# Gathering the low bits and the sign of 64-bit weights: 16-bit halves in place of 32-bit words

## The chip, the cores and the metric

The kernel runs on one core of one Trainium2 chip. The metric is the time of one execution in microseconds of the device, and the median of the runs shown is 682.36 us (three runs, 682.13 to 684.18). The core's engines run side by side and meet through semaphores: TensorE (PE, with its weight loads as PEld), VectorE (DVE), ScalarE (ACT), GpSimd (POOL) and SyncE (SP), which issues all of this kernel's DMAs.

## The reference, cut to what matters

```python
# attention: 4 batches, 8 heads, 768 positions, head size 64
k_sum = k.reshape(B, H, nb, block, D).max(axis=3)      # 24 blocks of 32 keys
v_sum = v.reshape(B, H, nb, block, D).mean(axis=3)
scores_l = where(|i - j| < 16, scale * q @ k.T, -1e9)  # a window
scores_s = scale * q @ k_sum.T + log(32)               # the block summaries
a = softmax(concat(scores_l, scores_s)); x = a @ concat(v, v_sum)
# feed-forward: 3072 tokens, 512 -> 2048 -> 512
h = x @ w_in
g = h * tanh(log1p(exp(min(h, 20))))                   # mish
return (g @ w_out).astype(float32)
```

The two weight matrices w_in and w_out arrive in 64-bit floating point (viewed as 64-bit integers), and the kernel makes 32-bit floats of them on the chip before it can multiply with them.

## The kernel before, in words

**Attention** is cut into units: a unit is one chunk of 256 queries of one batch and one pair of heads. There are 12 chunks and 4 pairs, so 48 units. A unit is loaded, scored on PE (lines 293 to 299), masked and reduced to its maximum on DVE (line 308, result `nm`), exponentiated on ACT (line 313, sums `sm`), scaled by the reciprocal of its sum (DVE lines 322 and 323 make `rs`, POOL line 324 multiplies), transposed on PE (line 330, copied out by ACT at line 332), and multiplied with the values on PE (line 348, split into a high and a low part by ACT line 349 and DVE line 350).

**Feed-forward** goes over six groups of 512 tokens (two chunks each) and 16 slices of 128 hidden columns, which gives 96 steps. A step is `ff_in` (12 matmuls, line 362), the activation on ACT (line 369), a split into high and low parts (lines 378 and 380) and, two steps later, `ff_out` (12 matmuls, line 390). Every product is made of three matmuls of high and low parts, so each weight is needed as a high part and a low part.

**Weights** come in 16 pieces of two 128x512 blocks, w_in and w_out in turn. A piece goes through five functions. `load_weight` (line 119) issues two DMAs into one of two staging buffers. `begin_weight` has ACT scale the upper 32-bit words into `f` (line 143) and has DVE gather, in the lower words `x`, what `f` lacks: the top three bits of the low word and the sign (lines 144 and 145). `join_weight` clamps `f` (line 154) and shifts the gathered bits in (line 156). `upper_weight` rounds that to the high part on ACT (line 129), and `lower_weight` subtracts to get the low part on DVE (line 134). `f` has one buffer, so the next piece's line 143 waits for line 134.

**Order.** Nothing reorders the program: each engine executes its instructions in the order in which the code writes them. There are two stages in which weights are prepared. In the first (about 0 to 55 us) the eight attention units of the first group run in a loop over u = 0 to 9: `begin_weight` stands at even u and `join_weight` at odd u, so five pieces are begun there. In the second (about 55 to 153 us), the first group's feed-forward steps run, and every step takes the weights on by one: upper and lower of the piece joined in the step before, then begin and join of the next. The other eleven pieces are begun in steps 0 to 10. A step with an attention unit (the even steps here) has on DVE, one behind the other: line 134, line 308 (four times), lines 144 and 145, lines 322 and 323, lines 154 and 156. A step without one has line 350 or nothing where lines 322 and 323 stand. From 153 us on the weights are ready and the other five groups run.

Of the kernel before, what the change touches and what calls it, by code (L numbers as in the profile page):

```python
# [9 lines left out]
F32 = mybir.dt.float32  # L10
F32R = mybir.dt.float32r
U32 = mybir.dt.uint32
I64 = mybir.dt.int64
AF = mybir.ActivationFunctionType
ALU = mybir.AluOpType
# [29 lines left out]

OFFSET = 112
F32_MAX = (0x47EFFFFF - (OFFSET << 23))
SIGN = 0x80000000


def _as_f32(bits):
    import struct
    return struct.unpack("<f", struct.pack("<I", bits))[0]
# [3 lines left out]
def fused_kernel(ctx: ExitStack, tc: tile.TileContext, q0, qk, kt, v0, vw, vs, w_in, w_out, out):  # L57
    nc = tc.nc
# [20 lines left out]
    for h in range(2):  # L79
        r = slice(h * QT, (h + 1) * QT)  # L80
        nc.gpsimd.affine_select(
            out=base[r, 0:KW], in_=base[r, 0:KW], pattern=[[1, KW]], base=-1,
            channel_multiplier=-1, compare_op=ALU.is_ge, fill=NEG / SCALE)
        nc.gpsimd.affine_select(
            out=base[r, 0:KW], in_=base[r, 0:KW], pattern=[[-1, KW]], base=2 * WIN - 1,
# [28 lines left out]
    def load_weight():  # L114
        if weights:
            w, fc = weights.pop(0)
            t = stage.tile([P, WB, WP], I64, tag="stage", name=f"w{w}_{fc}")
            for k in range(WB):
# [17 lines left out]
    def begin_weight():  # L136

        if loaded:
            w, fc, t = loaded.pop(0)
            words = t.rearrange("p k f -> p (k f)").bitcast(U32).rearrange("p (f two) -> p f two", two=2)  # L140
            x, high = words[:, :, 0], words[:, :, 1]
            f = ff.tile([P, WB * WP], F32, tag="f", name=f"w{w}_{fc}_f", bufs=1)
            nc.scalar.activation(f, high.bitcast(F32), AF.Copy, scale=2.0 ** -OFFSET)  # L143
            nc.vector.tensor_scalar(out=x, in0=x, scalar1=29, scalar2=None, op0=ALU.logical_shift_right)
            nc.vector.scalar_tensor_tensor(out=x, in0=high, scalar=SIGN, in1=x,
                                           op0=ALU.bitwise_and, op1=ALU.bitwise_or)
            begun.append((w, fc, f, x))

    def join_weight():

        if begun:
            w, fc, f, x = begun.pop(0)
            u = f.bitcast(U32)
            nc.vector.tensor_scalar(out=f, in0=f, scalar1=-_as_f32(F32_MAX), scalar2=_as_f32(F32_MAX),  # L154
# [13 lines left out]
    for part, step, at0 in ((blocks[:, :NQ], QT, -WIN), (blocks[:, NQ:], P, CH)):  # L168
        n = part.shape[1]
        nc.gpsimd.affine_select(  # L170
            out=part, in_=part, pattern=[[step, n], [-BLK, NB]], base=at0, channel_multiplier=1,
            compare_op=ALU.is_ge, fill=0.0)
        nc.gpsimd.affine_select(
            out=part, in_=part, pattern=[[-step, n], [BLK, NB]], base=BLK - 1 - at0, channel_multiplier=-1,
# [3 lines left out]
        out=part, in_=part, pattern=[[0, NQ], [0, NB]], base=-WIN, channel_multiplier=1,  # L178
        compare_op=ALU.is_ge, fill=0.0)
    nc.gpsimd.affine_select(  # L180
        out=part, in_=part, pattern=[[0, NQ], [0, NB]], base=WIN + QT - 1, channel_multiplier=-1,
# [200 lines left out]
    def ff_out(g, fc):  # L382
# [4 lines left out]
        for t in range(TG // P):  # L387
# [4 lines left out]
            if fc == NFC - 1:  # L392

                if t == 0:
                    res = stage.tile([P, WB, WP], I64, tag="stage", name=f"o{g}").bitcast(F32)
                    res = res.rearrange("p k f -> p (k f)").rearrange("p (t f) -> p t f", t=TG // P)
# [28 lines left out]
    for u in range(n + 2):  # L425
# [5 lines left out]
        if u % 2:  # L431
            join_weight()
        else:
            lower_weight()
            begin_weight()
# [27 lines left out]
    for i in range(len(steps) + 2):  # L463
# [12 lines left out]
        if i in at:  # L476
            att_scores(*at[i])
        begin_weight()
        if lower and i < NFC:
            lower()  # L480
# [61 lines left out]
```

## Time and profile before

| what | value |
|---|---|
| median of three runs | 682.36 us (682.13 to 684.18) |
| span of the profiled execution | 682.7 us (no other time is listed for it) |
| PE busy, DVE busy, ACT busy, POOL busy | 644.8, 291.2, 333.7, 66.3 us |
| line 144, 16 instructions | 11.1 us, 693 ns mean |
| line 145, 16 instructions | 19.6 us, 1227 ns mean |
| line 154, 16 instructions | 15.2 us, 951 ns mean |
| line 156, 16 instructions | 19.8 us, 1235 ns mean |

The span counts from the first to the last instruction. A busy share over the whole span says little here, because the first 153 us are built of other work than the rest; the stages have to be read one by one. In the lines of the profile, `w` is a staging buffer, `w_f` the scaled piece `f`, `w_early_..` and `w_late_..` the finished parts, `pr` the probabilities, `sc` their scores in PSUM, `ph` and `po` the sums of `ff_in` and `ff_out`. A name such as L145 is line 145 of the kernel before.

### The profile page before, as it was taken

The numbers are of one execution on the slowest core, as the hardware profiler recorded it, in microseconds if no ns is written. First come the engines' busy times: TensorE is split into PE (matmuls) and PEld (weight loads), VectorE is DVE, ScalarE is ACT, GpSimd is POOL, SyncE is SP. The second block draws the span as 40 slices with busy tenths as digits, with TensorE's granted clock in tenths as the row PEclk, the third lists the DMA queues.
The fourth block names the chain that finished last, engine by engine and source line by source line (L and its number), as shares of the span: only waits on it lengthen the run. The fifth ranks groups of instructions, "written<-read, shape, count | busy, mean of one in ns | idle before, by whom it ended". The sixth has DMA issues, their size and how long they took to land.

```text
span 682.7 us, 11000 instructions
## 1 busy us (share of the span) xinstructions
PE 644.8 (94%) x4224; PEld 516.0 (76%) x4224; DVE 291.2 (43%) x836; ACT 333.7 (49%) x722; POOL 66.3 (10%) x115
## 2 busy tenths in 40 slices
PE   4766989889999999999999999999999999999997
PEld 3655767667788788788788788788788788888886
DVE  3687889983242244452232244442242232221112
ACT  2576677777554454454454454454454454211111
POOL 3121100112010010010010010010010010000000
PEclk9876999999999999999999999999999999999999
DMA  8587446653141125351121135341141110010001
GB/s 284 157 235 231 155 161 222 240 173 106 46 150 46 45 68 159 100 191 46 45 89 45 45 130 158 103 128 46 45 151 44 45 60 1 13 50 1 0 1 62
DMA packets 32852, 69.54 MB, mean 102 GB/s; under 512 B 6944, under 2 KB 12064, under 8 KB 32800
## 3 DMA queue, kind: packets, MB, share of 16 engines
q1 hardware_dynamic: 32800, 68.84, 31.6%
q8 instruction: 33, 0.54, 0.3%
q14 instruction: 19, 0.16, 0.1%
HBM read 60.03 MB, written 6.29 MB: 97 GB/s over the span
## 4 chain that ended last, share of the span: by engine, by line
PE 80%; ACT 9%; DVE 5%; DMA 3%; issue 1%; SPq 0%
PE po L390 36%; PE ph L362 34%; PE x_ps L348 4%; PE sc L293 3%; PE pt_ps L330 2%; DVE w_f L156 2%; ACT w_f L143 2%; DVE w_f L154 2%; ACT pr L313 1%; PE vm_ps L239 1%; ACT L369 1%; ACT L313 1%; DMA vw<-vw 1%; DMA vw<-vm 1%; ACT a L369 1%
## 5 line engine op out<-in xcount | busy, mean ns | idle before, releaser
L369 ACT ACTIVATE a<-ph 128x512 f32<-128x512 f32 x96 | 57.4, 598 | 154.0 <-PE ph L362 153.6
L378 DVE CAST ah<-a 128x512 fp32r<-128x512 f32 x80 | 34.0, 425 | 197.0 <-ACT a L369 197.0
L390 PE MATMUL po<-w_early_out_hi,ah 128*128 128x512 f32 x240 | 98.3, 409 | 0.0
L362 PE MATMUL ph<-xh,w_early_in_hi 128*128 128x512 f32 x240 | 97.4, 406 | 0.0
L369 ACT ACT_TABLE_LOAD x41 | 52.6, 1283 | 88.6 <-PE ph L362 88.4
L390 PE MATMUL po<-w_early_out_lo,ah 128*128 128x512 f32 x240 | 95.0, 396 | 0.0
L390 PE MATMUL po<-w_early_out_hi,al 128*128 128x512 f32 x240 | 94.9, 395 | 0.0
L362 PE MATMUL ph<-xh,w_early_in_lo 128*128 128x512 f32 x240 | 94.9, 395 | 0.0
L362 PE MATMUL ph<-xl,w_early_in_hi 128*128 128x512 f32 x240 | 94.7, 395 | 0.0
L324 POOL TENSOR_TENSOR pr<-pr,rs 128x480 f32<-128x480 f32 x48 | 48.2, 1005 | 435.5 <-DVE rs L323 370.8
L313 ACT ACTIVATE pr<-pr,nm 128x120 f32<-128x120 f32 x192 | 73.5, 384 | 11.4 <-DVE nm L308 10.9
L350 DVE TENSOR_TENSOR xl<-x_ps,xh 128x256 fp32r<-128x256 f32 x48 | 20.3, 423 | 118.1 <-ACT xh L349 118.0
L380 DVE TENSOR_TENSOR al<-a,ah 128x512 fp32r<-128x512 f32 x96 | 66.3, 691 | 2.7
L390 PE MATMUL po<-w_late_out_hi,ah 128*128 128x512 f32 x144 | 58.0, 403 | 0.0
L362 PE MATMUL ph<-xh,w_late_in_hi 128*128 128x512 f32 x144 | 57.6, 400 | 0.0
L390 PE MATMUL po<-w_late_out_lo,ah 128*128 128x512 f32 x144 | 56.3, 391 | 0.0
L362 PE MATMUL ph<-xh,w_late_in_lo 128*128 128x512 f32 x144 | 56.2, 390 | 0.0
L362 PE MATMUL ph<-xl,w_late_in_hi 128*128 128x512 f32 x144 | 56.1, 390 | 0.0
L390 PE MATMUL po<-w_late_out_hi,al 128*128 128x512 f32 x144 | 56.0, 389 | 0.0
L390 PEld LDWEIGHTS po<-w_early_out_hi,ah 128*128 128x128 f32 x240 | 45.6, 190 | 12.9 <-issue 4.0
L390 PEld LDWEIGHTS po<-w_early_out_lo,ah 128*128 128x128 f32 x240 | 45.9, 191 | 10.3
L362 PEld LDWEIGHTS ph<-xh,w_early_in_lo 128*128 128x128 f32 x240 | 45.8, 191 | 10.1
(74 smaller groups left out, 927.5 us busy)
## 6 DMA issues: line engine op xcount, KB each, us to landing
qk<-qk SPq DMA_DIRECT2D x40, 496.0 KB
vw<-vw SPq DMA_DIRECT2D x48, 192.0 KB
w<-w_in SPq DMA_DIRECT2D x16, 512.0 KB
w<-w_out SPq DMA_DIRECT2D x16, 512.0 KB
ks<-kt SPq DMA_DIRECT2D x17, 384.0 KB
out<-o SPq DMA_DIRECT2D x24, 256.0 KB
vsum<-vs SPq DMA_DIRECT2D x12, 384.0 KB
vw<-vm SPq DMA_DIRECT2D x48, 48.0 KB
```

The source lines that it names most:

```text
L143: nc.scalar.activation(f, high.bitcast(F32), AF.Copy, scale=2.0 ** -OFFSET)
L154: nc.vector.tensor_scalar(out=f, in0=f, scalar1=-_as_f32(F32_MAX), scalar2=_as_f32(F32_MAX), op0=ALU.max, op1=ALU.min)
L293: nc.tensor.matmul(ps[h][row, at0:at0 + KA], u["qk"][r, s, h * QT:(h + 1) * QT], u["qk"][r, s, P:], start=True, stop=True)
L313: nc.scalar.activation(pr[:, s, :], pr[:, s, :], AF.Exp, scale=-1.0, bias=nm[:, s:s + 1], accum_out=sm[:, s:s + 1])
L324: nc.gpsimd.tensor_mul(pr, pr, rs.unsqueeze(2).broadcast_to([P, NQ, KA]))
L348: nc.tensor.matmul(x, u["v"][:, s, d], pt, start=True, stop=True)
L350: return lambda: nc.vector.tensor_sub(xl, ps[:, :CH], xh.bitcast(F32))
L362: nc.tensor.matmul(ph, w[:, cc * P:(cc + 1) * P], x[:, cc, :], start=(cc == 0 and n == 0), stop=(cc == NCC - 1 and n == 2))
L369: nc.scalar.activation(a, st[g, fc], AF.Mish)
L378: (nc.scalar.copy if g == 0 else nc.vector.tensor_copy)(ah, a)
L380: return lambda: nc.vector.tensor_sub(al, a, ah.bitcast(F32))
L390: nc.tensor.matmul(po[g][t], a[:, tok], w, start=(fc == 0 and n == 0), stop=(fc == NFC - 1 and n == 2))
```

## The change

The low word of a weight, seen as 16-bit halves, lies in halves 0 and 1, the high word in halves 2 and 3. The shift of line 144 put the top three bits of the low word at its bottom, and the two-input operation of line 145 then or-ed the sign of the high word into the top bit. Now half 0 receives half 1 shifted right by 13, and then half 1 receives half 3 masked with 0x8000. The low word holds the same 32 bits afterwards. Both instructions read one tensor, of 16-bit elements at a distance of four elements (8 bytes); each still passes over 1024 elements per partition. The rest of the program is as it was; the lines behind `begin_weight` stand three further down.

```diff
+U16 = mybir.dt.uint16
...
-SIGN = 0x80000000
+SIGN = 0x8000
...
             nc.scalar.activation(f, high.bitcast(F32), AF.Copy, scale=2.0 ** -OFFSET)
-            nc.vector.tensor_scalar(out=x, in0=x, scalar1=29, scalar2=None, op0=ALU.logical_shift_right)
-            nc.vector.scalar_tensor_tensor(out=x, in0=high, scalar=SIGN, in1=x,
-                                           op0=ALU.bitwise_and, op1=ALU.bitwise_or)
+            half = t.rearrange("p k f -> p (k f)").bitcast(U16).rearrange("p (f four) -> p f four", four=4)
+            nc.vector.tensor_scalar(out=half[:, :, 0], in0=half[:, :, 1], scalar1=13, scalar2=None,
+                                    op0=ALU.logical_shift_right)
+            nc.vector.tensor_scalar(out=half[:, :, 1], in0=half[:, :, 3], scalar1=SIGN, scalar2=None,
+                                    op0=ALU.bitwise_and)
             begun.append((w, fc, f, x))
```

No instruction changes its place on any engine. This is VectorE's list in one late step with an attention unit, at the sixth piece of w_out (`w_10`), before:

```order
L144 TENSOR_SCALAR w_10_1019<-w_10_1019 128x1024
L145 SCALAR_TENSOR_TENSOR w_10_1019<-w_10_1019 128x1024
L322 TENSOR_SCALAR rs_3_1150<-sm_3_1141 128x4
L323 RECIPROCAL rs_3_1150<-rs_3_1150 128x4
L154 TENSOR_SCALAR w_10_f<-w_10_f 128x1024
L156 SCALAR_TENSOR_TENSOR w_10_f<-w_10_f,w_10_1019 128x1024
```

and with the change:

```order
L146 TENSOR_SCALAR w_10_1019<-w_10_1019 128x1024
L148 TENSOR_SCALAR w_10_1019<-w_10_1019 128x1024
L325 TENSOR_SCALAR rs_3_1150<-sm_3_1141 128x4
L326 RECIPROCAL rs_3_1150<-rs_3_1150 128x4
L157 TENSOR_SCALAR w_10_f<-w_10_f 128x1024
L159 SCALAR_TENSOR_TENSOR w_10_f<-w_10_f,w_10_1019 128x1024
```

Only the second row is another kind of instruction; what stands behind it is the same work, in the same order.

## The prediction

> **What bounds the kernel now.** I read the stages first, then the chain of waits, then each engine's timeline where the chain passes. Busy times by stage (start:end, length, then PE, PEld, DVE, ACT, POOL busy, granted clock, DMA share, GB/s):
>
> ```profile
> 98.00:153.00 55.00, 49.86 (x302) 38.12 (x300) 51.27 (x84) 38.98 (x67) 6.51 (x7) 0.97 0.57 193
> 153.00:682.00 529.00, 525.74 (x3266) 424.17 (x3266) 170.22 (x579) 233.53 (x510) 42.56 (x67) 1.00 0.23 72
> ```
>
> From 153 us on PE is busy 525.74 of 529.00 us, and no weight is prepared there: nothing is to be gained behind 153 us, and what is gained ahead of it moves the end by as much. Between 98 and 153 us DVE is the fullest engine (51.27 of 55.00 us), which alone suggests that every DVE nanosecond counts. The chain says otherwise (start, length, what):
>
> ```profile
> 114.14 1.50 DVE w_f L154
> 115.64 0.02 issue
> 115.66 1.24 DVE w_f L156
> 116.90 0.02 issue
> 116.92 1.05 ACT w_late_out_hi L129
> ...
> 152.72 0.50 ACT pt L332
> 153.22 0.04 issue
> 153.26 0.64 PE sc L293 x14
> ```
>
> Step after step it runs from ACT's line 143 to DVE's lines 154 and 156 and back to ACT's line 129, then through ACT to the next line 143. The two instructions that change, lines 144 and 145, are not in it there. They run while ACT works towards line 143, and DVE then waits for that:
>
> ```profile
> DVE w_f L154 <- ACT w_f L143: 4.0, 11, 0.6
> ```
>
> In the second stage all eleven pieces find DVE waiting ahead of line 154, 4.0 us in total, 0.36 us each. There is one place where the changed lines do carry the chain, late in the first stage:
>
> ```profile
> 46.50 0.61 DVE w L144
> 47.11 0.02 issue
> 47.14 1.23 DVE w L145
> 48.37 0.33 DVE xl L350
> ...
> 53.15 1.76 DVE w_early_out_lo L134
> 54.91 0.02 issue
> 54.93 1.17 ACT w_f L143
> ```
>
> From line 144 to line 156 DVE (in the gap shown as "...") runs through without a pause, ACT's line 129 waits for its end, DVE's line 134 for that, and ACT's line 143 for line 134 (`f` has one buffer).
>
> **What the two instructions cost.** Both now read one tensor of 16-bit elements 8 bytes apart. The trace has no 16-bit instruction of this shape; it has these two (idle time ahead of them last):
>
> ```profile
> L145 DVE SCALAR_TENSOR_TENSOR w<-w 128x1024 uint32<-128x1024 uint32 x16 | 19.6, 1227 | 0.5
> L144 DVE TENSOR_SCALAR w<-w 128x1024 uint32<-128x1024 uint32 x16 | 11.1, 693 | 1.5 <-DMA w<-w_in 1.5
> ```
>
> Both pass over 1024 words that lie 8 bytes apart, and the one-input one takes 693 ns, the two-input one 1227. Bounds for the new instruction: 693 ns from the one-input row, 1227 from the other, if narrow elements lose the faster pace. A gain below 693 is excluded as long as elements are not taken in fours, and neighbours in memory are not neighbours in this stream. I take 693: kind, count and distance in bytes are those of line 144, only the width differs. So the shift stays at 0.69 us, the mask falls from 1.23 to 0.69, and a piece is **0.53 us shorter on DVE**; at the other bound it is 0.53 us longer, the shift then costing 1.23.
>
> The Trainium skill ("VectorE: DVE Perf Modes", section "What auto-detection actually checks") gives the pairing of 16-bit elements only for a step of one element, and the mode with both ports to any one-source instruction in SBUF with an even or matching count; by it both new instructions run two elements a cycle, as line 144 does, and the sum stays. No run here shows it for 16-bit elements.
>
> **Part 1: the pieces of the first stage.** The piece at 46.50 us moves everything behind it by **0.53 us**: its followers on DVE wait for nothing, and the chain from line 156 over lines 129, 134 and 143 to PE shifts whole. At the other four I cost the edit at nothing, because the next thing on DVE waits for PE, or ACT waits for `ff_in`:
>
> ```profile
> 16.61 0.28 DVE L308 CUSTOM_DVE_ANT_0 pr<-sc,first 128x120 f32<-128x120 f32 x1 [4.50 <-PE sc L299]
> 31.30 0.28 DVE L308 CUSTOM_DVE_ANT_0 pr<-sc,first 128x120 f32<-128x120 f32 x1 [4.61 <-PE sc L299]
> 44.46 0.28 DVE L308 CUSTOM_DVE_ANT_0 pr<-sc,base 128x120 f32<-128x120 f32 x1 [1.32 <-PE sc L299]
> 62.58 0.60 ACT L369 ACTIVATE a<-ph 128x512 f32<-128x512 f32 x1 [1.17 <-PE ph L362]
> ```
>
> All four covers are longer than 0.53 us. Without them it would be 0.53 us each, 2.1 us more.
>
> **Part 2: the steps without attention (odd).** DVE only waits longer for line 143: nothing.
>
> **Part 3: the steps with attention.** Here the changed lines stand ahead of lines 322 and 323, which release POOL's multiplication, and line 154 suffers when it runs beside that. An early step:
>
> ```profile
> 66.80 0.17 DVE L322 TENSOR_SCALAR rs<-sm 128x4 f32<-128x4 f32 x1 [0.76 <-ACT pr L313]
> 67.79 1.09 DVE L154 TENSOR_SCALAR w_f<-w_f 128x1024 f32<-128x1024 f32 x1 [0.62 <-ACT w_f L143]
> 67.35 0.99 POOL L324 TENSOR_TENSOR pr<-pr,rs 128x480 f32<-128x480 f32 x1 [12.33 <-DMA qk<-qk]
> ```
>
> and a late one, with ACT's last exponential ahead of line 143:
>
> ```profile
> 112.40 1.23 DVE L145 SCALAR_TENSOR_TENSOR w<-w 128x1024 uint32<-128x1024 uint32 x1
> 113.54 0.16 DVE L322 TENSOR_SCALAR rs<-sm 128x4 f32<-128x4 f32 x1
> 114.14 1.49 DVE L154 TENSOR_SCALAR w_f<-w_f 128x1024 f32<-128x1024 f32 x1 [0.23 <-ACT w_f L143]
> 112.87 0.18 ACT L313 ACTIVATION_READ_ACCUMULATOR pr<-pr,nm 128x1 f32 x1
> 114.09 0.99 POOL L324 TENSOR_TENSOR pr<-pr,rs 128x480 f32<-128x480 f32 x1 [7.29 <-DVE rs L323]
> ```
>
> Early, line 322 waits for ACT, POOL starts 0.55 us behind it, and line 154 shares 0.55 us with POOL (67.79 to 68.34) and takes 1.09 us. Alone it takes 0.69:
>
> ```profile
> 121.88 0.69 DVE L154 TENSOR_SCALAR w_f<-w_f 128x1024 f32<-128x1024 f32 x1 [0.20 <-ACT w_f L143]
> ```
>
> Late, the sums for the next batch (lines 229 and 249) have pushed DVE back, and line 322 waits for line 145, not for ACT, whose sum was there at 113.05. POOL starts 0.05 us ahead of line 154, shares 0.94 us with it, and line 154 takes 1.49. With the mask 0.53 us shorter, line 322 can start at about 113.1 (ACT now ends last), POOL 0.55 us later at 113.65, ending at 114.64; line 154 still starts at 114.14, shares 0.50 us and takes about 1.07, nearly as in the early step. That is **0.42 us off the chain**, for lines 156 and 129 follow at once. Two more steps look alike:
>
> ```profile
> 130.06 1.52 DVE L154 TENSOR_SCALAR w_f<-w_f 128x1024 f32<-128x1024 f32 x1 [0.19 <-ACT w_f L143]
> 146.03 1.51 DVE L154 TENSOR_SCALAR w_f<-w_f 128x1024 f32<-128x1024 f32 x1 [0.20 <-ACT w_f L143]
> ```
>
> So 3 x 0.43 = 1.3 us. In the three early steps line 322 waits for ACT already: nothing.
>
> **The sum:** 0.53 + 1.3 = 1.8 us off a span of 682.7, so 680.9; the median of the runs is 0.3 us below that span, so by it 682.36 - 1.8 = **680.6 us**.
>
> **The rivals.**
>
> *The narrow elements lose the faster pace* (slower). Both instructions take 1.23 us, a piece is 0.53 us longer. For it: no 16-bit row. Against it: the distance in bytes is that of line 144. Price: 0.53 at 46.50 us; in the second stage the eleven pieces are late by 11 x 0.53 less the 4.0 us of waiting, about 1.9 us; and in two early steps where line 322 waits only 0.18 us (one row below) POOL starts 0.35 us later into line 154, 0.7 us. Together 3.1 us: 685.5. It decides from 0.36 us a piece on; below that DVE's waiting hides it.
>
> ```profile
> 82.02 0.17 DVE L322 TENSOR_SCALAR rs<-sm 128x4 f32<-128x4 f32 x1 [0.18 <-ACT pr L313]
> ```
>
> *Narrow elements are slower still.* If each access of half a word cost half as much again as line 145's pace, 1.84 us, a piece would be 1.76 us longer, and twelve pieces less 4 us of waiting give 17 us: 699. Line 144 stepping 8 bytes at 693 ns speaks against any price of the step itself. The Trainium skill ("Vector Engine (DVE) Microarchitecture Reference", section "5.2 Measured stream behaviour on trn2 (trn3 not measured)") would have it so: full rate only for runs of two adjacent words, about 1.7 ns per element where a stream hops each element. By that figure an estimate of 1.8 us an instruction, but line 144 hops as well, and the trace does not agree.
>
> *The gain does not arrive.* The 0.53 us at 46.50 us is swallowed by a transfer that lands when it lands, and line 154 in the late steps meets POOL as before, or POOL takes the pair of ports later instead. Then 682.0, no change.
>
> *DVE is the bound where it is fullest.* If the waits of 0.2 us ahead of line 154 are only jitter, each of the six pieces from 98 to 153 us gives its 0.53 us: 3.2 + 0.53 = 3.7, so 678.7. For it stand the 51.27 of 55.00 us; against it, that ACT's own chain would not shorten with it.
>
> **How the numbers follow.** My forecast has 60 in 100, the lost pace 15, slower still 3, no gain arriving 13, DVE as the bound 9. A measurement of this kernel can tell 0.3% from no change, 2.05 us. The forecast's own range is 679.8 to 681.6, and about 0.45 of its chance lies beyond 2.05 us: faster 0.27 + 0.09 = 0.36; slower 0.15 + 0.03 = 0.18; the rest, 0.46, within. The range 678.6 to 685.6 goes from DVE as the bound to the lost pace, which are the bounds of the unknown price, and leaves out slower still and the ends of the others.
>
> **What would show it.** Right: the mask at about 690 ns, line 144's shift unchanged, DVE's busy time 8.5 us less (16 x 0.53); the three late clamps (lines 154 at 114, 130 and 146 us) near 1.08 us; the waits ahead of the clamps longer by some 0.5 us in odd steps; PE's unbroken run beginning near 151.4 us instead of 153.3. Wrong: either instruction above 0.7 us; the late clamps still at 1.5; the stage from 62 to 153 us as long as before; or a gain of several microseconds, which would mean that ACT's chain was not what held it.

## The result

The changed kernel takes 687.39 us (median of 15 runs, 685.04 to 688.89) against 682.51 for the kernel before, measured beside it (15 runs). The ratio is **1.0058, with a 95% interval of 1.0042 to 1.0074**: slower by 2.9 to 5.1 us. (Here and below the ratio is estimated over all the runs of a series; it is not the quotient of the two medians.) A second series gave 1.0042 (1.0024 to 1.0059). The forecast was 680.6, its range ended at 685.6.

The profiled execution of the change took 686.13 us, with a span of 684.4. In the groups of its DVE instructions (busy time, mean ns, idle time ahead) the changed pair has two rows:

```profile
L148 DVE TENSOR_SCALAR w<-w 128x1024 uint16<-128x1024 uint16 x16 | 21.3, 1329 | 0.5
L146 DVE TENSOR_SCALAR w<-w 128x1024 uint16<-128x1024 uint16 x16 | 21.1, 1322 | 2.4 <-DMA w<-w_in 2.4
```

Neither takes the 693 ns of the 32-bit shift. Both take longer than the two-input instruction that one of them replaced (1227 ns). DVE's busy time over the whole run is 300.6 us in place of 291.2, where 8.5 us less were forecast. The stages that answer to those quoted before:

```profile
98.00:153.00 55.00, 49.15 (x297) 37.52 (x296) 54.19 (x83) 36.92 (x64) 6.88 (x7) 0.97 0.54 183
```

DVE is busy for 54.19 of these 55 us (51.27 before). Its waits for ACT's line 143, which is line 144 in the changed kernel, have all but gone: 1.0 us at three of the eleven pieces, in place of 4.0 at all eleven.

```profile
DVE w_f L157 <- ACT w_f L144: 1.0, 3, 0.6
```

The chain of waits shows what that means (start, length, what). Before, it went over ACT at every step; now it stays on DVE from 99.64 us on, for 51 us:

```profile
102.24 1.22 DVE w_early_out_lo L135
103.46 1.27 DVE w L146
104.73 0.02 issue
104.75 1.32 DVE w L148
106.07 0.24 DVE xl L353
106.31 0.61 DVE w_f L157
106.92 0.02 issue
106.94 1.23 DVE w_f L159
...
150.51 0.02 issue
150.53 1.05 ACT w_late_out_hi L130
```

PE's unbroken run begins 1.7 us later than in the profile before, and what follows it is equally long (684.4 - 154.95 = 529.45 us; before 682.7 - 153.26 = 529.44):

```profile
154.95 0.64 PE sc L296 x14
```

The first stage ends at no fixed time, so the second is better measured from its first clamp (line 154 before, 157 now) to that instruction. Before it is 67.79 to 153.26, 85.47 us; now it is 66.78 to 154.95, **88.17 us, 2.7 us more**:

```profile
66.78 1.08 DVE L157 TENSOR_SCALAR w_f<-w_f 128x1024 f32<-128x1024 f32 x1 [0.62 <-ACT w_f L144]
```

### The profile page after: what moved, and what is told of

The parts are those of the page before. It is cut to its first block, busy times and chain, and to the rows that moved or that the text cites. A ratio compares the mean times of both kernels' runs of the same rounds, so it can differ in the third digit from the quotient of the medians.

```text
span 684.4 us, 11000 instructions
## 1 busy us (share of the span) xinstructions
PE 641.3 (94%) x4224; PEld 512.7 (75%) x4224; DVE 300.6 (44%) x836; ACT 333.7 (49%) x722; POOL 66.4 (10%) x115
## 4 chain that ended last, share of the span: by engine, by line
PE 79%; DVE 12%; ACT 4%; DMA 2%; issue 1%; SPq 0%; POOL 0%; POOLq 0%
PE po L393 35%; PE ph L365 33%; PE x_ps L351 3%; PE sc L296 3%; PE pt_ps L333 3%; DVE w_f L159 2%; DVE w L148 2%; DVE w L146 2%; DVE w_f L157 2%; DMA vw<-vw 1%; PE vm_ps L242 1%; DMA vw<-vm 1%; DVE pr L311 1%; ACT pr L316 1%; ACT L316 1%
```

## The experiments

Two theories stood against each other after this. One: the changed instructions are dear in themselves, and what the forecast said of a cheaper pair holds. The other: the gain would not have come even at the forecast price, because DVE's time is hidden or POOL takes it back. Within the first it was open why they are dear.

**What a 16-bit instruction costs alone.** Behind the kernel before, on idle buffers `pa` and `pb`, sixteen forms were executed four times each. `ah4` and `bh4` are 16-bit halves at a distance of four (8 bytes), `a2` and `b2` halves side by side, `ah2` at a distance of two, `aw2` and `bw2` 32-bit words at a distance of two. The lines shown here are 523 to 528, 531 and 535 of that kernel.

```diff
+    for _ in range(R): nc.vector.tensor_scalar(**shift(ah4[:, :, 0], ah4[:, :, 1]))
+    for _ in range(R): nc.vector.tensor_scalar(**shift(bh4[:, :, 0], ah4[:, :, 1]))
+    for _ in range(R): nc.vector.tensor_scalar(**shift(b2[:, :1024], ah4[:, :, 1]))
+    for _ in range(R): nc.vector.tensor_scalar(**shift(bh4[:, :, 0], a2[:, :1024]))
+    for _ in range(R): nc.vector.tensor_scalar(**shift(bh2[:, :, 0], ah2[:, :, 1]))
+    for _ in range(R): nc.vector.tensor_scalar(**shift(b2[:, :1024], a2[:, :1024]))
...
+    for _ in range(R): nc.vector.tensor_scalar(**shift(bw2[:, :, 0], aw2[:, :, 0], 29))
...
+    for _ in range(R): nc.vector.tensor_copy(bh4[:, :, 0], ah4[:, :, 1])
```

> The kernel before, followed by sixteen one-input and two-input VectorE instructions on idle staging buffers, four times each, with nothing else running. Theory A (16-bit elements at a distance lose the pace of two a cycle): 1024 elements of 16 bits at 8 bytes take 1.2 to 1.35 us in place and between two tiles alike, also as a plain copy; side by side they take well under 0.69 us; 32-bit words at 8 bytes stay at 0.69 us. Rival B (the distance of four elements is what costs, whatever the width): 32-bit words at four words are as slow per element as 16-bit halves at four, and 16-bit halves at a distance of two are fast. Rival C (writing half a word costs, reading does not): reading at a distance and writing side by side is fast, the reverse is slow. The rest of the run is the kernel before, so some 20 to 30 us more than 682.5 in all.

Groups of DVE instructions of that run:

```profile
L524 DVE TENSOR_SCALAR pb<-pa 128x1024 uint16<-128x1024 uint16 x4 | 5.2, 1308 | 0.1
L535 DVE COPY pb<-pa 128x1024 uint16<-128x1024 uint16 x4 | 5.2, 1301 | 0.1
L523 DVE TENSOR_SCALAR pa<-pa 128x1024 uint16<-128x1024 uint16 x4 | 5.2, 1301 | 5.7 <-DMA pa<-w_in 5.6
L526 DVE TENSOR_SCALAR pb<-pa 128x1024 uint16<-128x1024 uint16 x4 | 5.2, 1299 | 0.1
...
L527 DVE TENSOR_SCALAR pb<-pa 128x1024 uint16<-128x1024 uint16 x4 | 2.9, 735 | 0.1
...
L531 DVE TENSOR_SCALAR pb<-pa 128x1024 uint32<-128x1024 uint32 x4 | 2.8, 695 | 0.1
L525 DVE TENSOR_SCALAR pb<-pa 128x1024 uint16<-128x1024 uint16 x4 | 2.8, 694 | 0.1
...
L528 DVE TENSOR_SCALAR pb<-pa 128x1024 uint16<-128x1024 uint16 x4 | 1.7, 427 | 0.1
```

The form of the change takes 1301 ns with nothing else running, in place or between two tiles, as a shift or as a plain copy. So neither the other engines nor the place are the cause. Reading halves at 8 bytes and writing them side by side takes 694 ns (line 525), as the 32-bit shift does (line 531, 695). Reading side by side and writing at 8 bytes takes 1299 (line 526). **It is the writing of half words at a distance that costs**, the third of the expectations.

**By distance.** A second run of the same kind used 512 elements a form; `apart(t, n, s)` takes every s-th of them. Lines 520 to 525 write 16 bits at 2, 4, 6, 8, 12 and 16 bytes, line 526 reads them at 16 and writes them side by side, lines 527 to 530 write 32 bits at 4, 8, 12 and 16 bytes, and lines 535, 533 and 534 are the two-input form with 16 bits written at 2, 8 and 16 bytes.

```diff
+    for _ in range(R): nc.vector.tensor_scalar(**shift(b2[:, :512], a2[:, :512]))
+    for _ in range(R): nc.vector.tensor_scalar(**shift(apart(b2, 512, 2), a2[:, :512]))
...
+    for _ in range(R): nc.vector.tensor_scalar(**shift(b2[:, :512], apart(a2, 512, 8)))
+    for _ in range(R): nc.vector.tensor_scalar(**shift(b4[:, :512], a4[:, :512]))
...
+    for _ in range(R): nc.vector.scalar_tensor_tensor(**both(apart(b2, 512, 4), a2[:, :512], a2[:, 512:1024]))
```

> The kernel before, followed by sixteen more VectorE forms on idle buffers, each over 512 elements, mostly written at a distance and read side by side. Theory (a half word that is written costs by its distance in bytes): with 16 bits 0.29 us side by side, 0.43 to 0.45 at 4 bytes, 0.73 at 8, 1.0 at 12, 1.3 at 16; read at 16 bytes and written side by side 0.43; 32-bit words 0.43 at 4 and 8 bytes, 0.62 at 16; the two-input form, one element a cycle, at 8 bytes with 16 bits also about 0.73. Rival (16-bit elements merely fall to one element a cycle): 0.69 to 0.73 at every distance from 8 bytes on, in the one-input and the two-input form alike.

```profile
L534 DVE SCALAR_TENSOR_TENSOR pb<-pa 128x512 uint16<-128x512 uint16 x4 | 9.7, 2422 | 0.1
L525 DVE TENSOR_SCALAR pb<-pa 128x512 uint16<-128x512 uint16 x4 | 5.2, 1299 | 0.1
L533 DVE SCALAR_TENSOR_TENSOR pb<-pa 128x512 uint16<-128x512 uint16 x4 | 5.2, 1293 | 0.1
...
L524 DVE TENSOR_SCALAR pb<-pa 128x512 uint16<-128x512 uint16 x4 | 4.1, 1017 | 0.1
L523 DVE TENSOR_SCALAR pb<-pa 128x512 uint16<-128x512 uint16 x4 | 2.9, 734 | 0.1
L535 DVE SCALAR_TENSOR_TENSOR pb<-pa 128x512 uint16<-128x512 uint16 x4 | 2.8, 692 | 0.1
L530 DVE TENSOR_SCALAR pb<-pa 128x512 uint32<-128x512 uint32 x4 | 2.5, 620 | 0.1
...
L526 DVE TENSOR_SCALAR pb<-pa 128x512 uint16<-128x512 uint16 x4 | 2.4, 611 | 0.1
L522 DVE TENSOR_SCALAR pb<-pa 128x512 uint16<-128x512 uint16 x4 | 2.4, 594 | 0.1
L529 DVE TENSOR_SCALAR pb<-pa 128x512 uint32<-128x512 uint32 x4 | 2.0, 508 | 0.1
L521 DVE TENSOR_SCALAR pb<-pa 128x512 uint16<-128x512 uint16 x4 | 1.8, 454 | 0.1
L528 DVE TENSOR_SCALAR pb<-pa 128x512 uint32<-128x512 uint32 x4 | 1.7, 428 | 0.1
L527 DVE TENSOR_SCALAR pb<-pa 128x512 uint32<-128x512 uint32 x4 | 1.7, 426 | 0.1
...
L520 DVE TENSOR_SCALAR pb<-pa 128x512 uint16<-128x512 uint16 x4 | 1.2, 294 | 7.5 <-DMA pb<-w_in 7.4
```

From 4 bytes on, each further 2 bytes between the half words that are written cost 140 ns per 512 elements (454, 594, 734; then 1017 and 1299 for 4 bytes more each). At 16 bytes a half word that is written thus costs 2.1 times the half word that is read there (611) and 2.1 times the word that is written there (620). Reading at 16 bytes is not free either (611 against 294 side by side). Words written at 8 bytes cost nothing extra (428), which is why line 144 of the kernel before gave no warning. The two-input form costs 1293 at 8 bytes and 2422 at 16: from 8 to 16 bytes it rises by 1129 ns where the one-input form rises by 565, half as much. So "one element a cycle" is refuted: it would be the same at each distance. The expectation also missed in one place, for the two-input form was expected near 0.73 us at 8 bytes. That one-input forms rise at half the pace of two-input ones fits with their still handling two elements at a time, but no run shows this directly. What the write side does with the distance, no run shows either.

**The forecast's price, without 16 bits.** The kernel before, with a second one-input instruction on words; it leaves the sign of the weights out.

```diff
-            nc.vector.scalar_tensor_tensor(out=x, in0=high, scalar=SIGN, in1=x,
-                                           op0=ALU.bitwise_and, op1=ALU.bitwise_or)
+            nc.vector.tensor_scalar(out=x, in0=x, scalar1=7, scalar2=None, op0=ALU.bitwise_and)
```

> The kernel before with the two-input instruction replaced by a one-input one on 32-bit words that masks the low word alone; it leaves the sign of the weights out. This gives the changed pair the price that was forecast, 0.69 and 0.69 us. The forecast's theory: 0.53 us at the piece near 46 us and 0.42 us in each of three late steps, 1.8 us less than before, about 680.7 against 682.5. Rival (the gain does not arrive anyway): 682.5, no change. Rival (DVE as the bound from 98 us on): 678.8.

Measured: 682.02 us against 682.46, ratio **0.9981 (0.9967 to 0.9995)**: 0.3 to 2.3 us faster, with the forecast's 1.8 inside and both rivals (no gain; 3.7 us) outside. The interval does not tell 1.8 us from the 1.3 us of part 3 alone; for that the profile is needed. The new instruction's group, and the first of the late clamps, which took 1.49 us before:

```profile
L145 DVE TENSOR_SCALAR w<-w 128x1024 uint32<-128x1024 uint32 x16 | 11.2, 698 | 0.5
```

```profile
112.70 1.07 DVE L153 TENSOR_SCALAR w_f<-w_f 128x1024 f32<-128x1024 f32 x1 [0.64 <-ACT w_f L143]
```

The late clamp is at the 1.07 us that were worked out. From the first clamp (66.45 us) to PE's scores at 150.49 us the second stage takes 84.04 us, 1.43 less than the 85.47 before, where 1.3 were forecast.

```profile
66.45 1.09 DVE L153 TENSOR_SCALAR w_f<-w_f 128x1024 f32<-128x1024 f32 x1 [0.62 <-ACT w_f L143]
```

```profile
150.49 0.63 PE L292 MATMUL sc<-qk 64*64 64x120 f32 x14 [0.99 <-ACT pt L331]
```

The other part of the forecast, 0.53 us at the piece near 46 us, did not arrive in this profile. DVE does reach the clamp 0.53 us sooner after the start of line 144 (2.80 us in place of 3.33). But from that start to ACT's line 143, which the whole 0.53 us had to move, it is 8.43 us (45.67 to 54.10). In the two profiles with an unchanged first stage it is 8.52 (the kernel before) and 8.44 (the run with the clamp ahead of POOL). Here PE waited for a transfer of values, and ACT reached line 143 behind PE's product:

```profile
52.67 1.12 PE L347 MATMUL x_ps<-pt,vw 120*64 120x64 f32 x16 [3.08 <-DMA vw<-vm]
```

That is what the prediction's rival "The gain does not arrive" said of this piece: a transfer that lands when it lands. It is one profile.

**Only the mask on halves.** The shift goes back to words; the result is the reference's.

```diff
-            nc.vector.tensor_scalar(out=half[:, :, 0], in0=half[:, :, 1], scalar1=13, scalar2=None,
-                                    op0=ALU.logical_shift_right)
+            nc.vector.tensor_scalar(out=x, in0=x, scalar1=29, scalar2=None, op0=ALU.logical_shift_right)
```

> The change with its shift put back on 32-bit words; only the mask is on 16-bit halves. Theory A: 0.69 and 1.32 us, a piece 0.09 us longer than before, of which DVE's waits of 0.36 us per piece hide nearly all: 682.5 to 683.0. Rival (16-bit accesses disturb other engines, whatever they themselves take): half of the change's loss, 684.5.

Measured: 682.50 against 682.46, ratio 0.9986 (0.9966 to 1.0006). No loss, though the mask takes 1.33 us. In the profile the second stage, from the first clamp at 67.63 us to the scores at 152.67, takes 85.04 us, where the kernel before takes 85.47 and the change 88.17. So 16-bit accesses do no harm here beyond their own time, and the change's loss comes with the shift, which went from 0.69 to 1.32 us.

**The mask twice.** The change with one more 16-bit instruction in each piece.

```diff
             nc.vector.tensor_scalar(out=half[:, :, 1], in0=half[:, :, 3], scalar1=SIGN, scalar2=None,
                                     op0=ALU.bitwise_and)
+            nc.vector.tensor_scalar(out=half[:, :, 1], in0=half[:, :, 3], scalar1=SIGN, scalar2=None,
+                                    op0=ALU.bitwise_and)
```

> The change with its 16-bit mask executed twice (the second time it writes what is there already): one more VectorE instruction of 1.33 us in each of the 16 pieces. Theory (VectorE has become the bound from the second stage on, so that every further microsecond on it is paid in full): twelve pieces x 1.33 us, about 16 us more than the change, 702 to 704. Rival (ACT's chain still sets the pace and the change's loss lies elsewhere): well under half of that, below 694.

Measured: 703.48 us (two runs), 17.9 us above the change of the same series (685.57, below). The expected 702 to 704 is met, but not by twelve pieces. The profiled span is 701.3 us, 16.9 more than the 684.4 of the change's first profile, and the first clamp of the second stage (70.80 in place of 66.78) and the scores (171.86 in place of 154.95) divide this. Ahead of the clamp lie 4.0 us, as much as three pieces. Behind it lie 12.9 us, in which ten pieces are begun: 1.29 us a piece, nearly the 1.32 us that the instruction takes. So once its waits are used up, time on DVE is paid almost in full. In its waits for the clamp next to nothing is left:

```profile
DVE w_f L159 <- ACT w_f L144: 0.3, 1, 0.3
```

**The change once more**, for a second profile.

> The change itself once more, for a second profile. Theory: the second stage again takes some 93.4 us between the first clamp's step and PE's unbroken run, 2.7 us more than before, and the rest of the 4 us lies in the first stage, whose length differs between executions by a microsecond or so. Time 1.004 to 1.007 of before. Rival (the loss lies behind 153 us): the part behind the weights longer than the 529.4 us of before.

Measured: 685.57 against 683.18, ratio 1.0042 (1.0024 to 1.0059). From the first clamp at 66.09 us to the scores at 154.28 us it is 88.19 us, as in the first profile (88.17) and 2.7 more than before. (The 93.4 us of the expectation count from an earlier point, which it does not fix; the 2.7 us can be compared.) But 685.3 - 154.28 = 531.0 us follow, 1.6 us more than the 529.4 expected. The stretches behind that point, in the second profile of the change and in the first (the granted clock stands third from the end: 0.56 and 1.00), show where it goes:

```profile
154.00:157.50 3.50, 3.22 (x20) 2.44 (x21) 3.00 (x12) 3.44 (x9) 0.58 (x1) 0.56 0.46 151
```

```profile
155.00:158.50 3.50, 3.50 (x27) 2.85 (x28) 2.65 (x11) 3.44 (x9) 0.63 (x1) 1.00 0.36 111
```

In the second profile PE came out of its last waits with half the clock and did 20 matmuls where 27 were done in the first. The change is not shown to be the reason. The profile of the run with only the mask on halves has the same dip, with 22 matmuls in the first 3.5 us and 531.1 us behind the scores:

```profile
152.67:156.17 3.50, 3.50 (x22) 2.73 (x23) 2.80 (x11) 3.44 (x9) 0.81 (x1) 0.65 0.41 131
```

Yet PE's last two waits there (0.36 and 0.99 us) are no longer than in the kernel before (0.43 and 0.99), which came out of them at 1.00. The change's first profile waited longest (0.69 and 0.99) and came out at 1.00 too. Two of the eight profiles of whole kernels have this dip; what brings it on stays open.

**The clamp ahead of POOL.** In the kernel before, `join_weight` (lines 154 and 156) is put ahead of `att_normalize` in the second stage.

```diff
+        join_weight()
         if i in at:
             att_normalize(*at[i])
-        join_weight()
```

> The kernel before with lines 154 and 156 put ahead of lines 322 and 323 in the second stage, so that POOL's multiplication starts behind line 156 and not beside line 154. Theory (sharing with POOL is what stretches line 154): line 154 takes 0.69 us in all eleven pieces of that stage, six steps get 0.4 to 0.8 us shorter, some of it is given back where POOL then meets other DVE work: 2 to 3.5 us less than before, 679 to 680.5. Rival (the stretch moves with POOL to line 134 or 380 and comes back in full): 682.5.

Measured: 680.63 against 682.46, ratio **0.9966 (0.9953 to 0.998)**, 1.4 to 3.2 us faster: the fastest version here that keeps the whole weight. All eleven clamps of the stage take 0.68 or 0.69 us, which is 3.7 us less than before in all, and the stage (66.40 us to the scores at 149.51) is 2.4 us shorter, 83.11 us. So a part is given back. POOL now runs beside other DVE work: line 134 of the first five w_out pieces has a mean of 1508 ns in place of 1328. And PE waits for POOL ahead of each transpose, 11.6 us in six waits, where it was 2.8 us in two:

```profile
PE pt_ps L330 <- POOL pr L324: 11.6, 6, 5.5
```

**The same with the change.** The change with that order.

> The change with its lines 157 and 159 put ahead of lines 325 and 326 in the second stage, as in the run of the kernel before with the joining first. Theory (VectorE is the bound, and sharing with POOL costs it 0.4 to 0.8 us in six steps): 2 to 4 us less than the change, 682 to 685, at best level with the kernel before. Rival (with 16-bit elements POOL is not what costs): no gain over the change, 686.5.

Measured: 684.81 against 683.18, ratio 1.0025 (1.0006 to 1.0044); the change in the same series 1.0042. By the ratios that is 1.2 us of the expected 2 to 4 (0.8 by the medians), with intervals that overlap. In the profile the second stage (67.28 to 153.68) takes 86.40 us, 1.8 less than the 88.17 of the change; in the kernel before, the order took off 2.4. POOL meets line 135 here as it met line 134 there (1510 ns against 1508), so that does not explain a smaller gain, and whether the gain is smaller at all is not settled. It does not make the change level with the kernel before.

```profile
L135 DVE TENSOR_TENSOR w_early_out_lo<-w_f,w_early_out_hi 128x1024 fp32r<-128x1024 f32 x5 | 7.5, 1510 | 1.0 <-ACT w_early_out_hi L130 1.0
```

## Why the prediction was wrong

**The step that failed is the price of the pair.** "I take 693: kind, count and distance in bytes are those of line 144, only the width differs." It is the width that matters, on the side that writes: 1301 ns alone, 1322 and 1329 in the kernel. The bounds failed too. The upper end, 1227 ns, rested on the idea that the worst case is one element a cycle. Both rows that gave the bounds are of 32-bit words, so they could bound no cost that only half words have. The rival "slower still" was the one that left this open, at 3 in 100; its 1.84 us an instruction is about as far above the measured 1.3 us as 0.69 us is below.

The Trainium skill's condition for the two-port mode ("VectorE: DVE Perf Modes", section "What auto-detection actually checks") holds as far as the trace goes: line 525 of the first probe, 16 bits read at 8 bytes, takes the 694 ns of that pace. That page of the Trainium skill says nothing of a price for what is written, and I read a mode as if it were a duration.

The Trainium skill's other page ("Vector Engine (DVE) Microarchitecture Reference", section "5.2 Measured stream behaviour on trn2 (trn3 not measured)") warned of lone elements, about 1.7 ns each. I set it aside because line 144 hops as well. For words at 8 bytes that was right (428 ns, against 426 side by side, line 527 of the second probe). For half words written there the measured 1301 ns are 1.3 ns an element, so in number the warning was nearer than my figure. But that section gives it for 32-bit streams, and for reading as well as for writing; line 525 of the first probe, which only reads half words apart, takes 694 ns, 0.68 an element. So the nearness is luck.

**What the pair then costs.** From start to start the mask costs less than its duration says, since the next instruction begins before it has ended:

```profile
111.97 1.33 DVE L146 TENSOR_SCALAR w<-w 128x1024 uint16<-128x1024 uint16 x1
113.33 1.35 DVE L148 TENSOR_SCALAR w<-w 128x1024 uint16<-128x1024 uint16 x1
114.46 0.21 DVE L325 TENSOR_SCALAR rs<-sm 128x4 f32<-128x4 f32 x1
```

The mask holds its successor up for 1.13 us (113.33 to 114.46), as the two-input instruction did (112.40 to 113.54, 1.14). The shift holds it up for 1.36 us (111.97 to 113.33), where its 693 ns and the gap behind them made 0.72. A piece is thus about 0.6 us longer, all of it the shift's, in agreement with the run that has only the mask on halves. This is close to the 0.53 us of the first rival, for another reason than it named: by luck, since the rival had both instructions at 1.23 us.

**Part 3 and the lost pace.** The rival's sum for the second stage was 1.9 + 0.7 = 2.6 us (11 x 0.53 less 4.0 is 1.8, which makes it 2.5); measured are 2.7. Its mechanism is in the profile: the clamps that wait for ACT fall from eleven to three, and DVE becomes the bound. POOL's part in two early steps came as that rival had it: line 325 is late, POOL starts just ahead of the clamp, and the clamp takes 1.49 and 1.51 us in place of 1.08.

```profile
82.10 1.49 DVE L157 TENSOR_SCALAR w_f<-w_f 128x1024 f32<-128x1024 f32 x1 [0.22 <-ACT w_f L144]
98.09 1.51 DVE L157 TENSOR_SCALAR w_f<-w_f 128x1024 f32<-128x1024 f32 x1 [0.20 <-ACT w_f L144]
```

In the three late steps it came out otherwise than I thought. The clamp now goes ahead of POOL and is short; line 159, the former line 156, bears the overlap instead:

```profile
114.83 0.66 DVE L157 TENSOR_SCALAR w_f<-w_f 128x1024 f32<-128x1024 f32 x1
115.52 1.89 DVE L159 SCALAR_TENSOR_TENSOR w_f<-w_f,w 128x1024 uint32<-128x1024 uint32 x1
```

That the totals agree to 0.1 us is partly luck. The rival counted eleven pieces of 0.53 us; between the two marks ten pieces of 0.63 us are begun, 6.3 us, of which the 3.0 us of waits that vanished hide nearly half. POOL's share and smaller waits make the rest of the way to 2.7, and I have not added them up.

**What held.** Behind the weights nothing is gained or lost in one profile of the change; the other loses 1.6 us there by PE's clock, which the prediction had not thought of. The chain's reading was right for the second stage: with the price that I had assumed, the gain comes, 1.43 us where 1.3 were forecast, with the late clamps at 1.07. For the piece near 46 us it was not borne out: the one profile with that price lost the 0.53 us to a transfer. "DVE is the bound where it is fullest" was rightly a rival, since only 0.36 us of waiting a piece stood between the kernel and that state.

**What stays open.** 2.7 us of the loss are shown in the second stage. The two series give 2.9 to 5.1 and 1.6 to 4.0 us. Another 0.6 us is seen at the piece near 46 us. From the start of line 146 to ACT's line 144 it is 9.11 us (45.35 to 54.46) and 9.07 in the change's two profiles, where the kernel before and the clamp ahead of POOL have 8.52 and 8.44:

```profile
54.46 1.15 ACT L144 ACTIVATE w_f<-w 128x1024 f32<-128x1024 f32 x1 [1.31 <-DVE w_early_out_lo L135]
```

How much of it reaches the end cannot be read from the totals. The profiles reach their first clamp at 67.79 us in the kernel before and at 66.40 with the clamp ahead of POOL, which has the same first stage, so that stage differs by more from execution to execution. The 1.6 us of PE's clock, in one profile of two, is not shown to come from the change.

## What to carry to other kernels

Take the price of an instruction from a row of the same width on the side that it writes, or measure it alone before the change is built on it; four executions behind the kernel on an idle buffer were enough here. To replace one two-input instruction by a cheaper one, look at what else in the pair has to change with it: here the shift, without which nothing was lost. An engine with 0.36 us of waiting a piece hides no more than that, and what lies above it comes through almost whole: 1.29 of 1.32 us a piece with the mask twice.

## What the runs showed of the hardware

VectorE writes half words that lie apart at a price set by their distance: with 512 elements and one input 454 ns at 4 bytes, 734 at 8, 1299 at 16, and with two inputs 1293 at 8 and 2422 at 16. Reading them apart costs much less (694 ns for 1024 elements at 8 bytes, 611 for 512 at 16), and writing them side by side least (294 for 512). A one-input instruction on 32-bit floats that shares its time with a POOL multiplication of 0.99 us takes 1.49 us in place of 0.69, and with the clamp ahead of POOL it takes 0.69. That exchange of order gained 1.4 to 3.2 us, about what the change was meant to gain (1.8). PE's granted clock was 0.56 and 0.65 over the 3.5 us behind its last waits in two of eight profiles, after waits of 0.65 and 0.99 and of 0.36 and 0.99 us; after waits of 0.69 and 0.99 and of 0.43 and 0.99 us it was 1.00 in two others.
